# A Fourier-mixing and squared-ReLU kernel: other weights for the pieces of the next transform, products and helpers issued at other places

## The chip, the cores and the metric

The kernel runs on one core of a Trainium2 chip. Its engines are TensorE (matrix products), VectorE and GpSimd (elementwise work), ScalarE (activations and copies) and SyncE, whose queue (SP's) starts most transfers. Each engine works through its own list of instructions in order and waits on semaphores for the others. The metric is the time on the device in microseconds; lower is better.

## The reference

The input x has 8 sequences of 3008 rows and 256 columns. Each is transformed by a two-dimensional Fourier transform of which the real part is kept; the rows that result go through a feed-forward layer with a squared ReLU:

```python
X = np.fft.fft(x, axis=1)
X = np.fft.fft(X, axis=2)
y = X.real.reshape(8 * 3008, 256)
h = y @ w_in              # 256 x 2048
r = np.maximum(h, 0.0)
out = (r * r) @ w_out     # 2048 x 256
```

## The kernel before

**The transform of a sequence** uses symmetry. Rows n, S-n, M-n and M+n are loaded together (`load_x`), and `fold` adds and subtracts them on VectorE in five pieces: `f_s`, `f_d`, `f_sc`, `f_dc` and `f_w`, and for three of the eight tiles a sixth, a reversal of the partitions. Pairs of tiles are then halved further by turns (`once`, `twice`): copies and scaled copies on ScalarE (`begin`, `sine`, `copies`) and sums on VectorE (`even`, `odd`, `turned`, `odd_v`, `odd_w`). What the turns multiply by lies in the small tile `turn`, made by `make_turn` from columns of the tables of cosines and sines. Last come four groups for each sequence (`dft_ops`, `group`; part P or Q, even or odd columns). Each has a product `even_n` on TensorE, joins on VectorE, a second product `odd_n`, and `join_1`, which writes Pt or Qt. The products go to PSUM tiles `pd` of a pool with two buffers, which `even_n` and `odd_n` use in turn, so an `even_n` may start when the group before has joined the even half. ScalarE copies part of a product to SBUF ahead of each join.

One column of every transform (E) is treated apart. `load_column` fetches it for sequences 1 to 7 during steps 8 to 14 in 28 small transfers, `fold_columns` doubles it on ScalarE and folds it on VectorE into `we`, and a pass of two groups, `dft_ops(None)`, transforms it; the result is stored to `e_dram` and later broadcast to Et (`load_e`). After this pass `part_table` reorders the columns of four tables on ScalarE; the pass needs the old order, the groups of sequences 1 to 7 the new one.

**The main loop** goes through 384 steps: 8 sequences, 6 blocks of 251 (the last 250) columns, and 8 steps j in each. A step's `front` makes, for two halves h, two products into PSUM `ph` (two buffers; L763 and L764) and from these on VectorE `he` and both sides of `g` (L766, L768, L769); `combine` applies ReLU and square on ScalarE (L778, L779) and makes four sums s on GpSimd (L786 to L789). `back` makes seven products from g and s into accumulators in PSUM, two steps later (LAG is 2). The first eight steps are of a plainer form, and w_out is converted during them. After a block's last step `gather` combines the accumulators, and `store` transposes and stores in two later steps.

**The next sequence's transform is woven in.** `ahead(b + 1)` lists its pieces, each with a cost. After each half of a front `between` is called. It lowers `spent` by `pace` (the sum of costs by the number of calls; a quarter of it before step 16), and then issues pieces while `spent` is not above zero, adding their costs:

```python
while side and spent <= 0:
    t, f = side.pop(0)
    f()
    spent += t
```

Nothing is issued in the first ten steps nor in steps with i % 8 == 1. An issued piece stands in its engines' queues behind what was issued before it: a product issued in the first half's call stands on TensorE between the two halves of that front, a piece for VectorE right after that half's g. So the costs decide in which half step a piece stands and nothing else. In sequence 0 there are 53 calls, later 78.

Of the kernel before, what the change touches and what calls it, by code (L numbers as in the profile page):

```python
# [82 lines left out]
def kernel(  # L83
# [12 lines left out]
    nc = tc.nc  # L96
    B, NROW, _, D = x.shape
# [6 lines left out]
    NJ = NFC // 2  # L104
# [33 lines left out]
    ODD0 = NT - 3  # L138
    TWO = ODD0 - 2
# [44 lines left out]
    cosT = const.tile([P, 2, WT], F32, name="cosT")  # L184
    sinT = const.tile([P, 2, WT], F32, name="sinT")
# [150 lines left out]
    turn = const.tile([P, 3, 4], F32, name="turn")  # L336
    BY_AC, BY_BD, BY_TWO, BY_AB = range(4)

    def make_turn():


        for i, t, kp, k in ((BY_AC, ODD0, 1, 0), (BY_TWO, TWO, 1, 0), (BY_AB, ODD0, 0, 1)):
            for a, tab in enumerate((cosT, sinT, sinT)):
                r = slice(0, ROWS2)
                nc.scalar.mul(turn[r, a, i:i + 1], tab[r, kp, PLACE[t] + k:PLACE[t] + k + 1], -1.0 if a == 2 else 1.0)
        c, z = (turn[0:ROWS2, a, BY_AC:BY_AC + 1] for a in range(2))
        for a, (u, v, op) in enumerate(((c, z, ALU.add), (c, z, ALU.subtract), (z, c, ALU.subtract))):
            to = turn[0:ROWS2, a, BY_BD:BY_BD + 1]
            tt(out=to, in0=u, in1=v, op=op)
            nc.scalar.mul(to, to, 0.5 ** 0.5)  # L350
# [35 lines left out]
    def load_column(t):  # L386

        _, r0, step, rows = TILES[t]
        for i in range(4):
            nc.sync.dma_start(out=xe[0:rows, i, t], in_=x[1:B, r0:r0 + step * (rows - 1) + 1:step, i, H].rearrange("b r -> r b"))  # L390

    def fold_columns():
        nc.scalar.mul(xe, xe, 2.0)
        s = hp.tile([P, 2, NT, NE], F32, name="es", tag="es", bufs=1)
        tt(out=s, in0=xe[:, 0::2], in1=xe[:, 1::2], op=ALU.add)
        for kp in range(2):
            tt(out=we[:, kp], in0=s[:, 0], in1=s[:, 1], op=ALU.subtract if kp else ALU.add)
# [3 lines left out]
    def fold(b, t):  # L401


        odd, two = b > 0 and t >= ODD0, b > 0 and t == TWO + 1
        r = slice(0, ROWS2 if odd or two else TILES[t][3])
        st = {}

        def new(pool, nm, shape):
            st[nm] = pool.tile(shape, F32, name=nm, tag=nm)
            return st[nm]  # L410

        def f_s():
            nonlocal folds
            st["fs"] = sums[folds % 2]
            folds += 1
            v = xt[b, t]
            tt(out=st["fs"][r, :, 0:D], in0=v[r, 0::2], in1=v[r, 1::2], op=ALU.add)

        def f_d():
            v = xt[b, t]  # L420
            tt(out=new(fp, "fd", [P, 2, D])[r], in0=v[r, 0::3], in1=v[r, 1:3], op=ALU.subtract)
            if b > 0:
                load_later(b * NL + ORDER.index(t) + NX)

        def halves():

            if b == 0 or "sc" not in st:
                st["sc"] = fp.tile([P, 2, D], F32, name="sc", tag="sc")
            return st["sc"]

        def f_sc():
            s = st["fs"]
            tt(out=halves()[r, :, PART[0]], in0=s[r, :, 0:H + 1], in1=s[r, :, D:H - 1:-1], op=ALU.add)

        def f_dc():
            d = st["fd"]
            tt(out=halves()[r, :, PART[1]], in0=d[r, :, 1:H], in1=d[r, :, D - 1:H:-1], op=ALU.subtract)

        def w_of(t):
            if (b, t) not in folded:  # L440
                folded[b, t] = wp.tile([P, 2, D], F32, name="w", tag="w")
            return folded[b, t]

        def f_w(part=slice(0, D)):
            v, w = st["sc"], w_of(t)
            for kp in range(2):
                tt(out=w[r, kp, part], in0=v[r, 0, part], in1=v[r, 1, part], op=ALU.subtract if kp else ALU.add)

        def f_e():
            nc.scalar.mul(lone[r, 2 * t:2 * t + 2, P - 1:], w_of(t)[r, :, H:H + 1], -1.0 if TILES[t][0] else 1.0)  # L450

        if b == 0:
            return [f_s, f_d, f_sc, f_dc, lambda: (f_w(PART[0]), f_e()), lambda: f_w(PART[1])]
        ops = [(0.9, f_s), (0.9, f_d), (0.7, f_sc), (0.6, f_dc), (1.1, f_w)]
        if odd and (t - ODD0) in (1, 2) or two:
            ops.append((0.7, lambda: nc.vector.stream_shuffle(w_of(t)[r], w_of(t)[r], REVERSE)))
        return ops

    def spare(nm):
# [77 lines left out]
    def dft_ops(b):  # L537
# [7 lines left out]
        def group(kp, which):  # L545
# [168 lines left out]
            if b == 0:  # L714
# [3 lines left out]
                    for nm, f in (("even", even_part), ("odd", odd_part)):  # L718
                        named += [(nm + ("", "_e")[e] + str(i), lambda i=i, e=e, f=f: f(i, e == 1)) for e in range(2)]
                return [((which, kp, nm), f) for nm, f in named]  # L720
            ops = [(0.1, even_n), (0.4, join_4), (0.5, join_2), (0.1, odd_n), (0.8, join_1)]
            if b and kp:
                ops.insert(4, (0.5, lambda: join_odd("odd", n0)))
                ops.insert(2, (0.4, lambda: join_odd("half", n1)))
            elif b:
                ops.insert(4, (0.4, join_turned))
            return ops

        ops = [] if b is None else [(0.0, start)]
# [19 lines left out]
    def load_e(b):  # L749
        nc.sync.dma_start(out=PQE[b][2], in_=e_dram[b:b + 1].to_broadcast([P, NKT]))  # L750
# [137 lines left out]
            nc.sync.dma_start(out=rows[full * R:], in_=part[R - rest:, full])  # L888

    def ahead(b):  # L890
        start, *groups = dft_ops(b)
        if b == 1:

            tables = [(0.3, lambda tab=tab, t=t: part_table(tab, t)) for t in (TWO, ODD0) for tab in (cosT, sinT)]
            groups = [(1.5, fold_columns)] + dft_ops(None) + tables + groups
        def woven(ops, chain):

            chain = list(chain)
            out = []
            for i, x in enumerate(ops):  # L900
                out += [x] + ([chain.pop(0)] if chain and i else [])
            return out + chain

        av, aw, bv, bw = range(ODD0, NL)

        def later(make):

            made = []

            def run(i):  # L910
                if not made:
                    made.extend(make())
                made[i]()

            return lambda times: [(x, lambda i=i: run(i)) for i, x in enumerate(times)]

        w = lambda t: folded[b, t]
        two = later(lambda: once(w(TWO), w(TWO + 1), BY_TWO))((0.1, 0.9, 0.2, 1.0))
        first = later(lambda: once(w(av), w(aw), BY_AC))((0.1, 0.9, 0.2, 1.0))
        second = later(lambda: once(w(bv), w(bw), BY_BD) + twice(w(av), w(aw), w(bv), w(bw)))(  # L920
            (0.1, 0.9, 0.2, 1.0, 0.1, 1.2, 0.2, 1.2, 0.2, 0.9, 0.9))
        return (fold(b, TWO) + fold(b, TWO + 1) + woven(fold(b, 0), two) + fold(b, av) + fold(b, aw)
                + woven(fold(b, bv), first) + fold(b, bw) + woven(fold(b, 1), second)
                + [start] + groups + [(0.0, lambda: load_e(b))])

# [95 lines left out]
    def between():  # L1023


        nonlocal spent
        if i < NJ + LAG or i % NJ == LAG - 1:
            return
        spent -= pace / 4 if i < 2 * NJ else pace
        while side and spent <= 0:  # L1030
            t, f = side.pop(0)
            f()
            spent += t

    late = []

# [20 lines left out]
    for i in range(len(steps) + LAG + 4):  # L1057
        if i < len(steps):
            b, k0, n, j = steps[i]
            if i == NJ:  # L1060
                for k in range(NX):
                    load_later(NL + k)
            if NJ <= i < NJ + NT:
                load_column(i - NJ)
            if i == NJ:
                make_turn()
            if i % per == 0:
                assert not side
                side = ahead(b + 1) if b + 1 < B else []
                calls = 2 * (NJ - 1) * (len(BLOCKS) - (0 if i else 2)) - 6 + (0 if i else (NJ - LAG) // 2)  # L1070
                spent, pace = 0.0, sum(t for t, _ in side) / calls
            g = front(b, k0, n, j, between)
            if i < NJ:
                weights()
                s = combine(n, g, True)
            elif i < 2 * NJ:
                leftover()
                sum_wout(j)
        while finished and finished[0][0] <= i:
            store(*finished.pop(0)[1:])  # L1080
        if i >= LAG and flight:
            at, g_, s_ = flight.pop(0)
            final = at[:3] == (B - 1, *BLOCKS[-1])
            back(at[2], at[3], g_, s_, final)
            if at[3] == NJ - 1:
                c_ = gather(at[2], s_ is None, final)
                finished += [(i + 2 + s, *at[:3], s, c_, final) for s in range(2)]
        if i + 1 < NJ:
            late.append(win[i + 1][2]())
            leftover()  # L1090
        if i < len(steps):
            flight.append(((b, k0, n, j), g, s if i < NJ else combine(n, g, False)))
# [63 lines left out]
```

## Time and profile before

| what | value |
|---|---|
| median of 3 runs | 1939.22 us (1937.83 to 1939.67) |
| the profiled execution | 1939.15 us |
| its span, first to last instruction | 1937.4 us |
| mean granted clock of TensorE | 0.998 |
| busy: TensorE, VectorE, GpSimd, ScalarE | 1916.4, 1498.2, 1178.7, 957.4 us |
| TensorE busy from 300 to 400 us | 100.00 us |

Step 8 begins at about 98 us, step 48 (sequence 1) at about 312 us, and each later sequence of 48 steps takes some 231 us. A line of the timeline gives the start in us, the duration, the engine, the line of the kernel, what is written from what, and in brackets how long the engine stood idle before it and for whom. TensorE's matmuls are pipelined: two that are shown with 0.59 us follow the next pair after 0.425 us. A list of waits gives the waiting engine and line, for whom, the total in us, how often, and the longest.

### The profile page before, as it was taken

The numbers are of one execution on the slowest core, as the hardware profiler recorded it, in microseconds if no ns is written. First come the engines' busy times: TensorE is split into PE (matmuls) and PEld (weight loads), VectorE is DVE, ScalarE is ACT, GpSimd is POOL, SyncE is SP. The second block draws the span as 40 slices with busy tenths as digits, with TensorE's granted clock in tenths as the row PEclk, the third lists the DMA queues.
The fourth block names the chain that finished last, engine by engine and source line by source line (L and its number), as shares of the span: only waits on it lengthen the run. The fifth ranks groups of instructions, "written<-read, shape, count | busy, mean of one in ns | idle before, by whom it ended". The sixth has DMA issues, their size and how long they took to land.

```text
span 1937.4 us, 28151 instructions
## 1 busy us (share of the span) xinstructions
PE 1916.4 (99%) x9266; PEld 1699.7 (88%) x9266; DVE 1498.2 (77%) x3657; ACT 957.4 (49%) x1201; POOL 1178.7 (61%) x1701
## 2 busy tenths in 40 slices
PE   8999999999999999999999999999999999999998
PEld 7788878888988889888988889888898888988887
DVE  8989967888778886888868887788877788655554
ACT  2845544455445454544544455445544455444443
POOL 0047645667566765676556766676756676556655
PEclk9999999999999999999999999999999999999999
DMA  8331102111111111111011210121112101100101
GB/s 216 115 37 44 40 8 52 30 28 32 33 29 36 31 27 27 36 31 43 12 36 29 45 28 11 37 45 28 28 17 49 35 12 22 27 12 11 22 11 23
DMA packets 145786, 69.58 MB, mean 36 GB/s; under 512 B 129309, under 2 KB 136423, under 8 KB 145638
## 3 DMA queue, kind: packets, MB, share of 16 engines
q1 hardware_dynamic: 145186, 66.87, 15.9%
q8 instruction: 73, 1.20, 0.3%
q14 instruction: 75, 0.61, 0.1%
q0 software_dynamic: 176, 0.65, 0.1%
q10 hardware_dynamic: 276, 0.26, 0.0%
HBM read 43.03 MB, written 24.69 MB: 35 GB/s over the span
## 4 chain that ended last, share of the span: by engine, by line
PE 93%; DVE 4%; DMA 1%; SPq 1%; issue 1%; ACT 0%; POOL 0%; DVEq 0%; POOLq 0%
PE mA L816 16%; PE mC L816 16%; PE mB L816 16%; PE ph L763 16%; PE ph L764 16%; PE mD L816 8%; PE pd L564 2%; PE pd L666 1%; PE pd L640 1%; DVE he L766 1%; DVE g L769 0%; DMA cosT<-in_cos_s_dram 0%; DVE m L284 0%; DVE g L768 0%; DVE fd L282 0%
## 5 line engine op out<-in xcount | busy, mean ns | idle before, releaser
L778 ACT ACTIVATE g<-g 128x1004 f32<-128x1004 f32 (+1 forms) x384 | 399.3, 1040 | 747.3 <-DVE g L769 315.6
L786 POOL TENSOR_TENSOR s<-g 128x251 f32<-128x251 f32 (+1 forms) x376 | 244.8, 651 | 652.7 <-ACT g L779 574.1
L766 DVE SCALAR_TENSOR_TENSOR he<-Et,gE,ph 128x251 f32<-128x251 f32 (+1 forms) x768 | 359.8, 468 | 314.5 <-PE ph L764 312.7
L763 PE MATMUL ph<-Pt,G 128*128 128x251 f32 (+1 forms) x1536 | 452.6, 376 | 3.5 <-DVE g L769 3.4
L764 PE MATMUL ph<-Qt,G 127*128 127x251 f32 (+1 forms) x1536 | 451.7, 375 | 0.0
L779 ACT ACTIVATE g<-g 128x1004 f32<-128x1004 f32 (+1 forms) x384 | 399.3, 1040 | 12.2
L816 PE MATMUL mC<-s,wsum 128*128 128x251 f32 (+1 forms) x1504 | 381.7, 375 | 0.0
L816 PE MATMUL mA<-g,wout 128*128 128x251 f32 (+1 forms) x1504 | 381.6, 375 | 0.0
L768 DVE TENSOR_TENSOR g<-he,ph 128x251 f32<-128x251 f32 (+1 forms) x768 | 320.5, 417 | 52.9 <-ACT g L778 0.5
L764 PEld LDWEIGHTS ph<-Qt,G 127*128 127x128 f32 x1536 | 291.5, 190 | 35.9
L763 PEld LDWEIGHTS ph<-Pt,G 128*128 128x128 f32 x1536 | 286.4, 189 | 40.3 <-DVE g L769 5.8
L816 PEld LDWEIGHTS mC<-s,wsum 128*128 128x128 f32 x1504 | 285.6, 190 | 34.7
L769 DVE TENSOR_TENSOR g<-he,ph 128x251 f32<-128x251 f32 (+1 forms) x768 | 314.2, 409 | 0.0
L816 PEld LDWEIGHTS mA<-g,wout 128*128 128x128 f32 x1504 | 281.8, 189 | 35.4 <-issue 1.3
L787 POOL TENSOR_TENSOR s<-s,g 128x251 f32<-128x251 f32 (+1 forms) x376 | 292.0, 776 | 29.5
L788 POOL TENSOR_TENSOR s<-g 128x251 f32<-128x251 f32 (+1 forms) x376 | 294.4, 783 | 0.0
L789 POOL TENSOR_TENSOR s<-g,s 128x251 f32<-128x251 f32 (+1 forms) x376 | 257.8, 686 | 0.0
L816 PE MATMUL mB<-g,wsum 128*128 128x251 f32 (+1 forms) x752 | 220.7, 374 | 0.0
L816 PE MATMUL mD<-s,wout 128*128 128x251 f32 (+1 forms) x752 | 220.3, 374 | 0.0
L816 PE MATMUL mB<-s,wout 128*128 128x251 f32 (+1 forms) x752 | 219.9, 374 | 0.0
L816 PEld LDWEIGHTS mB<-g,wsum 128*128 128x128 f32 x752 | 142.9, 190 | 17.5
L816 PEld LDWEIGHTS mD<-s,wout 128*128 128x128 f32 x752 | 141.9, 189 | 17.7
(152 smaller groups left out, 1442.3 us busy)
## 6 DMA issues: line engine op xcount, KB each, us to landing
out_dram<-os SPq DMA_DIRECT2D x376, 56.0 KB
xt<-in_x_dram SPq DMA_DIRECT2D x39, 384.0 KB
xt<-in_x_dram SPq DMA_DIRECT2D x63, 128.0 KB
Et<-e_dram SPq DMA_DIRECT2D x7, 752.5 KB
out_dram<-os SPq DMA_DIRECT2D x288, 6.8 KB
raw<-in_moe_w_in_dram SPq DMA_DIRECT2D x16, 256.0 KB
raw<-in_moe_w_out_dram SPq DMA_DIRECT2D x16, 256.0 KB
xt<-in_x_dram SPq DMA_DIRECT2D x2, 512.0 KB
```

Of the source, the lines that this page charges most:

```text
L763: nc.tensor.matmul(hP, G1[:, fs], pt[:, ks], start=True, stop=True)
L764: nc.tensor.matmul(hQ, G2[0:P - 1, fs], qt[0:P - 1, ks], start=True, stop=True)
L766: nc.vector.scalar_tensor_tensor(out=t, in0=et[:, ks], scalar=gE[:, fc:fc + 1], in1=hP, op0=ALU.mult, op1=ALU.add)
L768: tt(out=g[:, h, 0, 0:n], in0=t, in1=hQ, op=ALU.add)
L769: tt(out=g[:, h, 1, 0:n][:, ::-1], in0=t, in1=hQ, op=ALU.subtract)
L778: act(v, v, AF.Relu)
L779: act(v, v, AF.Square)
L786: gt(out=s1, in0=g21, in1=g22, op=ALU.add)
L787: gt(out=s2, in0=s1, in1=g11, op=ALU.subtract)
L788: gt(out=s3, in0=g11, in1=g21, op=ALU.subtract)
L789: gt(out=s4, in0=g12, in1=s2, op=ALU.subtract)
L816: nc.tensor.matmul(acc[nm][:, i, 0:n], w, v[:, 0:n], start=j == 0 and i == 0, stop=j == NJ - 1, skip_group_check=True)
```

## The change

The costs of the pieces are replaced by others. Pieces of cost zero are no longer counted: `between` issues them right after the piece ahead of them, in the same call, and ends its counted loop at them. The products `even_n` and `odd_n` and the ScalarE helpers of the turns (`begin`, `sine`, `copies`), which had 0.1 or 0.2, now have zero. `make_turn` is split: `take_turn` takes the nine factors, `make_turn` does the rest, and both stand at the head of sequence 1's list in place of step 8's start. The doubling of E's column becomes a piece of its own, and it, the fold, the pass for E and the four tables, which stood between the turns and the groups, now stand between the folds of the tiles av and aw, in the middle of the list. The tables have cost zero.

```diff
-    def make_turn():
+    def take_turn():
         for i, t, kp, k in ((BY_AC, ODD0, 1, 0), (BY_TWO, TWO, 1, 0), (BY_AB, ODD0, 0, 1)):
             for a, tab in enumerate((cosT, sinT, sinT)):
                 r = slice(0, ROWS2)
                 nc.scalar.mul(turn[r, a, i:i + 1], tab[r, kp, PLACE[t] + k:PLACE[t] + k + 1], -1.0 if a == 2 else 1.0)
+
+    def make_turn():
         c, z = (turn[0:ROWS2, a, BY_AC:BY_AC + 1] for a in range(2))
...
+    def scale_columns():
+        nc.scalar.mul(xe, xe, 2.0)
+
     def fold_columns():
-        nc.scalar.mul(xe, xe, 2.0)
         s = hp.tile([P, 2, NT, NE], F32, name="es", tag="es", bufs=1)
...
-        ops = [(0.9, f_s), (0.9, f_d), (0.7, f_sc), (0.6, f_dc), (1.1, f_w)]
+        ops = [(1.0, f_s), (0.9, f_d), (0.6, f_sc), (0.6, f_dc), (1.3, f_w)]
         if odd and (t - ODD0) in (1, 2) or two:
-            ops.append((0.7, lambda: nc.vector.stream_shuffle(w_of(t)[r], w_of(t)[r], REVERSE)))
+            ops.append((0.8, lambda: nc.vector.stream_shuffle(w_of(t)[r], w_of(t)[r], REVERSE)))
...
-            ops = [(0.1, even_n), (0.4, join_4), (0.5, join_2), (0.1, odd_n), (0.8, join_1)]
+            ops = [(0.0, even_n), (0.5, join_4), (0.8, join_2), (0.0, odd_n), (1.2, join_1)]
             if b and kp:
-                ops.insert(4, (0.5, lambda: join_odd("odd", n0)))
-                ops.insert(2, (0.4, lambda: join_odd("half", n1)))
+                ops.insert(4, (0.7, lambda: join_odd("odd", n0)))
+                ops.insert(2, (0.5, lambda: join_odd("half", n1)))
             elif b:
-                ops.insert(4, (0.4, join_turned))
+                ops.insert(4, (0.5, join_turned))
...
-        start, *groups = dft_ops(b)
+        (_, start), *groups = dft_ops(b)
         if b == 1:
 
-            tables = [(0.3, lambda tab=tab, t=t: part_table(tab, t)) for t in (TWO, ODD0) for tab in (cosT, sinT)]
-            groups = [(1.5, fold_columns)] + dft_ops(None) + tables + groups
+            tables = [(0.0, lambda tab=tab, t=t: part_table(tab, t)) for t in (TWO, ODD0) for tab in (cosT, sinT)]
+            early = [(0.0, start), (0.0, take_turn), (0.5, make_turn)]
+            middle = [(0.0, scale_columns), (2.0, fold_columns)] + dft_ops(None) + tables
+        else:
+            early, middle = [], []
+            groups = [(0.0, start)] + groups
...
-        two = later(lambda: once(w(TWO), w(TWO + 1), BY_TWO))((0.1, 0.9, 0.2, 1.0))
-        first = later(lambda: once(w(av), w(aw), BY_AC))((0.1, 0.9, 0.2, 1.0))
+        two = later(lambda: once(w(TWO), w(TWO + 1), BY_TWO))((0.0, 1.1, 0.0, 1.5))
+        first = later(lambda: once(w(av), w(aw), BY_AC))((0.0, 1.1, 0.0, 1.5))
         second = later(lambda: once(w(bv), w(bw), BY_BD) + twice(w(av), w(aw), w(bv), w(bw)))(
-            (0.1, 0.9, 0.2, 1.0, 0.1, 1.2, 0.2, 1.2, 0.2, 0.9, 0.9))
-        return (fold(b, TWO) + fold(b, TWO + 1) + woven(fold(b, 0), two) + fold(b, av) + fold(b, aw)
+            (0.0, 1.1, 0.0, 1.5, 0.0, 1.2, 0.0, 1.4, 0.0, 1.1, 1.1))
+        return (early + fold(b, TWO) + fold(b, TWO + 1) + woven(fold(b, 0), two) + fold(b, av) + middle + fold(b, aw)
                 + woven(fold(b, bv), first) + fold(b, bw) + woven(fold(b, 1), second)
-                + [start] + groups + [(0.0, lambda: load_e(b))])
+                + groups + [(0.0, lambda: load_e(b))])
...
-        while side and spent <= 0:
+        while side and side[0][0] and spent <= 0:
             t, f = side.pop(0)
             f()
             spent += t
+        while side and not side[0][0]:
+            side.pop(0)[1]()
...
-            if i == NJ:
-                make_turn()
```

## The prediction

> **What bounds the kernel now.** First the page's busy times, then the busy time of each engine in stretches of the run.
>
> ```profile
> PE 1916.4 (99%) x9266; PEld 1699.7 (88%) x9266; DVE 1498.2 (77%) x3657; ACT 957.4 (49%) x1201; POOL 1178.7 (61%) x1701
> ...
> 160.00:200.00 40.00, 39.50 (x186) 34.78 (x186) 37.42 (x86) 21.89 (x28) 27.32 (x37) 1.00 0.21 53
> 200.00:244.00 44.00, 42.45 (x198) 36.81 (x196) 41.50 (x98) 23.62 (x37) 28.37 (x40) 1.00 0.18 37
> 244.00:300.00 56.00, 53.28 (x270) 43.76 (x271) 38.55 (x110) 24.99 (x44) 23.69 (x37) 0.97 0.10 25
> ...
> 486.00:600.00 114.00, 114.00 (x568) 102.34 (x567) 85.13 (x215) 53.94 (x67) 71.40 (x104) 1.00 0.13 29
> 728.00:970.00 242.00, 242.00 (x1179) 216.41 (x1178) 191.90 (x466) 120.16 (x148) 156.88 (x224) 1.00 0.14 30
> ```
>
> The columns after the length are TensorE matmuls, weight loads, VectorE, ScalarE and GpSimd, then the granted clock. TensorE sets the time. From 300 us to the last sequence it has no idle time at all, so whatever the change does to the six later transforms can only cost. Only in the first sequence, up to about 300 us, is anything to be won; there VectorE is at 94% (41.50 of 44 us) and TensorE has holes. The chain of waits for TensorE names them:
>
> ```profile
> PE ph L763 <- DVE g L769: 3.4, 4, 1.6
> ...
> PE pd L564 <- DVE we L397: 2.7, 1, 2.7
> ...
> PE pd L564 <- DVE dc L608: 0.3, 1, 0.3
> ```
>
> Four waits for VectorE's g and one for the columns we. The timeline shows the two large ones. Near 104 us, where `make_turn` stands ahead of step 8's front:
>
> ```profile
> 102.83 1.04 ACT L779 ACTIVATE g<-g 128x1004 f32<-128x1004 f32 x1
> ...
> 103.77 0.19 ACT L345 ACTIVATE turn<-cosT 96x1 f32<-96x1 f32 x1
> ...
> 104.08 0.30 DVE L349 TENSOR_TENSOR turn<-turn 96x1 f32<-96x1 f32 x3 [3.96 <-ACT turn L345]
> 104.30 0.47 DVE L766 SCALAR_TENSOR_TENSOR he<-Et,gE,ph 128x251 f32<-128x251 f32 x1
> ...
> 105.60 0.69 PE L763 MATMUL ph<-Pt,G 128*128 128x251 f32 x2 [1.57 <-DVE g L769]
> ...
> 107.58 1.04 PE L764 MATMUL ph<-Qt,G 127*128 127x251 f32 x2
> ```
>
> VectorE sits 3.96 us for nine ScalarE factors that queue behind the squares; TensorE waits 1.57, then runs at half rate (1.04 where 0.59 is usual). And at 246 us:
>
> ```profile
> 245.21 0.43 DVE L395 TENSOR_TENSOR es<-xe 128x98 f32<-128x98 f32 x1
> ...
> 245.67 1.38 DVE L397 TENSOR_TENSOR we<-es 128x49 f32<-128x49 f32 x2
> ...
> 246.43 1.63 PE L564 MATMUL pd<-cosT,we 95*7 95x95 f32 x8 [2.67 <-DVE we L397]
> ...
> 247.99 2.04 PE L816 MATMUL mA<-g,wout 128*128 128x251 f32 x4
> ```
>
> The same again: 2.67 idle, then 2.04 for four matmuls that take 1.01.
>
> **What the Trainium skill says.** "TensorE: Matmul & The Clock Gate", Part 1, What's actually happening: the array falls to half clock after an idle window of about 3.4 us and needs as long a busy stretch to recover. The trace agrees on the recovery (slow until 110.5 and 250.5, some 4 us each) but differs on the trigger: 1.57 us was enough, while the 1.04 us at 237 was not. Same page, Architectural detail: ScalarE and VectorE are strict FIFOs, and TensorE may pull only weight loads forward; the 3.96 us, with step 8's front stuck behind L349, is that. "SBUF — State Buffer", two separate sides: VectorE with two SBUF inputs and GpSimd exclude each other; L492, always 94x256, runs from 0.474 to 0.934 us here, so traced costs of pieces scatter by a factor of two.
>
> **Where the pieces go.** The costs are only weights in the planner's count; they change positions, no instruction. For b=1 the sum before is 33.6 (eight folds of 4.2) + 2.1 (shuffles) + 11.3 (turns) + 1.5 + 3.8 (pass for E) + 1.2 (tables) + 10.2 (groups) = 63.7; after 35.2 + 2.4 + 12.6 + 0.5 + 2.0 + 5.0 + 0 + 13.4 = 71.1. Over 53 calls the pace is 1.202 and 1.342; the first 12 (steps 10 to 15) count a quarter. fold_columns has 47.0 ahead of it before: (47.0-12x0.3005)/1.202 = 36.1, so the 37th full call, first half of step 37; its products come a call later. After: 21.5 ahead, (21.5-4.02)/1.342 = 13.03, the 14th full call, second half of step 23, and as even_n now costs 0 it is issued **in the same call**. Likewise the last turn piece, and with it the first product of sequence 1, falls in step 38. For b>1: 57.2 and 63.6 over 78, pace 0.733 and 0.815; nothing overruns.
>
> **Part by part**, in TensorE time, counted between issues (a matmul pair is 0.425 us).
>
> 1. make_turn leaves step 8. The last issue before the hole ends at 103.87; six pairs (2.55) later would be 106.42, but it is 110.50. Lost 4.1, all of it freed unless something else is late next: the conversion of wout that the products need (0.68+0.69+0.69 behind two fronts of 1.2 from 100.1) ends near 104.6, before its use at 105.6. I take 4.1; the ends are 1.7 (idle alone) and 4.1. The factors come back in step 10: nine ScalarE copies (0.84 traced) then three subtractions (0.3) and three ScalarE scalings (0.37). ScalarE has a 1.25 us gap there. VectorE may wait some 0.6 for them with the first fold queued behind, and is 0.9 later through steps 11 to 15, where it does 4.77 us a step by its fronts against TensorE's 4.675. Cost 0.5 at step 16 (0 to 1.4).
> 2. The pass for E leaves step 37: lost from 243.49 (h1's last issue end) to 250.51. Of this 2.94 is the wait, and 1.73 the slow clock (products 1.56 for the 1.07 of the second pass's, mA 1.84 for 0.85, mB 0.68 for 0.425). Freed 4.7.
> 3. It arrives in step 23. There TensorE's front starts at 174.63 and both halves are issued by 1.70 later. VectorE starts that front 1.0 late (176.27 against 174.63+0.63), then needs front 1.22, f_w of av 1.11, front 1.24, and es and the first we 1.17 less 0.06: we is ready 0.63+1.0+4.68 = 6.3 after the step's start. Wait 4.6, against 2.94 before: the call of slack is gone. With the slow clock at its old 1.73: 6.3. Without any lag 5.3; with 2 us lag and a full slow window more, 8.3. The moved step's other instructions: the xe scaling on ScalarE (0.35, a call earlier, so done by 177.8 before VectorE asks); 28 column loads, issued by 144.9, so they have landed; 28 products (same count); the E store on SP's queue, behind which only stores of steps 27 and 28 stand; twelve table copies on ScalarE, now in one call of step 26. They took 3.7 us traced (260.64 to 264.33) beside half-idle ScalarE; the pair g and s of that step is used two steps (9.35 us) later and needs about 5. Hidden; without that cover up to 2.
> 4. The folds after it: 22 calls instead of 23 before the turns are done. The bunch of four butterflies and turned products (2.81 and 1.13 traced at 233 to 238, which cost the waits of 1.04 and 0.27) stays in adjacent calls, and the one at 166 (0.50) too: taken as unchanged, 2.6 in all; ends 0 and 4.
> 5. Groups: the 0.46 at 288 goes, but the second product group in step 39 now needs join_2 of the call before: TensorE ready 0.85+0.86+0.85 = 2.56 after the step's start, join_2 done near 0.63+1.24+1.16 = 3.0: 0.45 back. Net 0.
> 6. Later sequences: join_4 no longer stands in the call of its product, so VectorE waits less; VectorE bounds nothing there. The same PSUM reuse occurs twice in each (six sequences): join_2 alone is 0.62, so done at 2.50, against 2.56. Zero; ends 0 and 0.5 each.
>
> Sum: -4.1 + 0.5 - 4.7 + 6.3 = **-2.0 us**. The profiled execution is 1939.15 (span 1937.4, 1.75 around it), the median of the runs 1939.22: forecast **1937.2 us**. A change is told from none here at about 0.2%, 3.9 us.
>
> **Rivals.**
> - *Both holes close.* If VectorE reaches step 23 without lag (wait 3.6, sum 5.3) and real weights also spread the bunches (-2.6): -4.1+5.3-4.7-2.6 = -6.1, 1933.1. For it: weights come closer to traced times (f_s 0.96 in later sequences, was 0.9; join_1 1.1, was 0.8). Against: VectorE's total work in the first sequence is the same and near full.
> - *Slower: a product in TensorE's queue before its PSUM buffer is free.* Place: the second and fourth product group of every sequence, in the call after the join_2 that releases the buffer, with matmuls strictly in order behind it. Each us that VectorE is late counts fully, twelve times. Above 0.17 us each (12x0.17 = 2.0) it outweighs the forecast, at 0.5 it gives +4.0, at 0.8 +7.6 (1946.7). Against: before that call VectorE has 4.5 us of work in a step of 5.5.
> - *The make_turn gain doesn't arrive*: VectorE, not TensorE, paces steps 9 to 22, so that only 1.7 comes and stalls at 16 and 21 take 2.0: -1.7+2.0-4.7+7.3 = +2.9, 1942.0.
>
> **Chances.** Forecast as summed 0.48, both holes 0.25, PSUM order 0.12, no gain from make_turn 0.15. Faster by over 0.2% needs -3.9: the second case and a little of the first, 0.27. Slower by over 0.2%: most of the third case and a third of the last, plus a worse stall at step 23, 0.19. Within: 0.54. The likeliest case alone spans 1935 to 1940; the range that holds the rivals down to the last fifth is 1933.0 to 1944.0.
>
> **What would show it.** Right: no VectorE wait for turn near 100 us and matmuls of 0.59 from 99 to 110; the wait of TensorE for we grows from 2.7 to about 4.4 us and moves to around 170 us, with half-rate matmuls after it; stretches from 300 us on still without TensorE idle. Wrong: the wait for we under 3, a new row of pd waiting for joins with a count of twelve, or waits for VectorE's g above 3.

## The result and the profile after

The changed kernel takes 1951.67 us (median of 4 runs, 1949.55 to 1954.28) where the kernel before takes 1939.45: a ratio of 1.0064, 95% interval 1.0046 to 1.0081. It is slower, where 1937.2 us was forecast with a range of 1933.0 to 1944.0. The profiled executions are 1953.37 and 1939.15 us, their spans 1951.6 and 1937.4: 14.2 us apart, and it is these that the sums below explain. The profiled execution of the changed kernel is one of two that took some 4 us more than the other two, at a mean granted clock of 0.996 against 0.999, so its half-rate stretches need not be in every run.

The busy times of the changed kernel and two of its stretches (TensorE, weight loads, VectorE, ScalarE, GpSimd, clock):

```profile
PE 1925.7 (99%) x9266; PEld 1701.7 (87%) x9266; DVE 1510.8 (77%) x3657; ACT 952.6 (49%) x1201; POOL 1185.4 (61%) x1701
...
160.00:200.00 40.00, 35.13 (x148) 26.36 (x147) 26.07 (x62) 14.80 (x20) 17.75 (x26) 0.91 0.11 24
728.00:970.00 242.00, 241.44 (x1169) 214.90 (x1169) 191.78 (x464) 117.25 (x145) 157.91 (x224) 1.00 0.14 31
```

The stretch in which TensorE had no idle time before, 728 to 970 us, now has 0.56 us of it. By the starts of their first fronts, each of the six later sequences takes 232.74 us where it took 231.43. The waits of TensorE after the change (engine and line, for whom, total, times, longest):

```profile
PE ph L765 <- DVE g L771: 4.7, 6, 1.2
PE pd L566 <- DVE we L399: 3.5, 1, 3.5
...
PE pd L566 <- DVE dc L612: 2.1, 7, 0.8
PE pd L566 <- DVE dc L610: 1.7, 6, 0.3
PE pd L668 <- DVE Qt L610: 1.6, 1, 1.6
```

L765 and L771 are L763 and L769 of before. The last three rows are new in kind or in number: products into `pd` that wait for joins, 14 times where it was once. Laid out by place, with the half-rate matmuls that follow a long wait counted in (read off the starts of successive matmuls against the usual 0.425 us a pair):

| TensorE time lost, us | before | after |
|---|---|---|
| step 8, the factors | 4.1 | 0 |
| folds up to step 23, waits for g | 0.8 | 3.8 |
| the pass for E | 4.6 | 6.7 |
| folds and turns after it, waits for g | 1.8 | 3.0 |
| products of sequence 1's groups, waits for dc and Qt | 0.6 | 4.7 |
| six later sequences | 0 | 6 x 1.31 = 7.8 |
| sum | 11.9 | 26.0 |

The difference, 14.1, agrees with the 14.2 between the spans. By the starts of the fronts, 6.8 us are lost between steps 8 and 48 and 7.8 after that, and the start-up before step 8 was 0.5 shorter.

One of the longer waits for g comes after step 18 of the changed kernel:

```profile
148.78 0.93 DVE L435 TENSOR_TENSOR sc<-fs 96x258 f32<-96x258 f32 x1
149.63 0.84 DVE L439 TENSOR_TENSOR sc<-fd 96x254 f32<-96x254 f32 x1
150.50 1.59 DVE L449 TENSOR_TENSOR w<-sc 96x256 f32<-96x256 f32 x2
...
153.31 0.69 PE L765 MATMUL ph<-Pt,G 128*128 128x251 f32 x2 [1.14 <-DVE g L771]
```

f_sc, f_dc and f_w all stand in one call, between the two halves of the step. The new costs allow that: 0.6 and 0.6 together are under the pace of 1.342, so a third piece can follow, while the old 0.7 and 0.6 exceed the old pace of 1.202.

Where the pass for E stands now, in step 23:

```profile
177.56 0.41 DVE L771 TENSOR_TENSOR g<-he,ph 128x251 f32<-128x251 f32 x1
177.98 0.26 DVE L397 TENSOR_TENSOR es<-xe 128x98 f32<-128x98 f32 x1
178.27 0.33 DVE L399 TENSOR_TENSOR we<-es 128x49 f32<-128x49 f32 x2
178.54 2.06 PE L566 MATMUL pd<-cosT,we 95*7 95x95 f32 x8 [3.55 <-DVE we L399]
180.53 2.04 PE L818 MATMUL mA<-g,wout 128*128 128x251 f32 x4
182.37 1.04 PE L818 MATMUL mB<-g,wsum 128*128 128x251 f32 x2
...
184.04 1.43 PE L818 MATMUL mC<-s,wsum 128*128 128x251 f32 x4
```

The products follow the fold in the same call, so TensorE stands idle for 3.55 us in front of them, and after that runs at half rate until about 185 us. And one of the new waits, in step 84 of the changed kernel, at the second product group of a later sequence:

```profile
487.75 0.58 PE L765 MATMUL ph<-Pt,G 128*128 128x251 f32 x2
488.80 0.48 DVE L768 SCALAR_TENSOR_TENSOR he<-Et,gE,ph 128x251 f32<-128x251 f32 x1 [0.76 <-PE ph L766]
489.97 0.35 DVE L608 TENSOR_TENSOR dc<-db,pd 128x189 f32<-128x189 f32 x1
490.23 0.34 DVE L612 TENSOR_TENSOR dc<-db,pd 128x188 f32<-128x188 f32 x1
490.72 0.65 PE L566 MATMUL pd<-cosT,w 95*128 95x94 f32 x4 [0.21 <-DVE dc L612]
```

VectorE begins the front 1.05 us after TensorE's first issue, because its first instruction waits for both products (L766 in the bracket), not for the one it reads. join_2 (L608, L612) ends at 490.57, and only then may the product go that was ready at 490.34. Counted between issues this place costs 0.47 us, its twin in step 88 0.54.

The longest of the new waits is in step 43 of the first sequence, at the second product of the last group, and the matmuls after it run at half rate:

```profile
294.00 1.04 PE L668 MATMUL pd<-cosT,w 94*127 94x95 f32 x4 [1.63 <-DVE Qt L610]
```

### The profile page after: what moved, and what is told of

Read it like the earlier page. It is cut to its first block, busy times and chain, and to the rows that moved or that the text cites. A ratio compares the mean times of both kernels' runs of the same rounds, so it can differ in the third digit from the quotient of the medians.

```text
span 1951.6 us, 28139 instructions
## 1 busy us (share of the span) xinstructions
PE 1925.7 (99%) x9266; PEld 1701.7 (87%) x9266; DVE 1510.8 (77%) x3657; ACT 952.6 (49%) x1201; POOL 1185.4 (61%) x1701
## 4 chain that ended last, share of the span: by engine, by line
PE 87%; DVE 10%; issue 1%; DMA 1%; POOL 0%; SPq 0%; ACT 0%; DVEq 0%; POOLq 0%
PE mA L818 15%; PE mC L818 15%; PE mB L818 15%; PE ph L765 15%; PE ph L766 15%; PE mD L818 8%; PE pd L566 2%; DVE he L768 2%; DVE g L770 1%; DVE g L771 1%; DMA xt<-in_x_dram 1%; PE pd L668 1%; PE pd L642 1%; DVE w L449 0%; DVE w L471 0%
## 5 line engine op out<-in xcount | busy, mean ns | idle before, releaser
L788 POOL TENSOR_TENSOR s<-g 128x251 f32<-128x251 f32 (+1 forms) x376 | 243.2, 647 | 661.8 <-ACT g L781 527.1
L765 PE MATMUL ph<-Pt,G 128*128 128x251 f32 (+1 forms) x1536 | 453.8, 376 | 5.1 <-DVE g L771 4.7
L766 PE MATMUL ph<-Qt,G 127*128 127x251 f32 (+1 forms) x1536 | 451.8, 375 | 0.0
L765 PEld LDWEIGHTS ph<-Pt,G 128*128 128x128 f32 x1536 | 284.6, 189 | 45.6 <-DVE g L771 11.1
L766 PEld LDWEIGHTS ph<-Qt,G 127*128 127x128 f32 x1536 | 291.4, 190 | 35.7
L771 DVE TENSOR_TENSOR g<-he,ph 128x251 f32<-128x251 f32 (+1 forms) x768 | 314.3, 409 | 0.0
L790 POOL TENSOR_TENSOR s<-g 128x251 f32<-128x251 f32 (+1 forms) x376 | 305.3, 812 | 0.0
L789 POOL TENSOR_TENSOR s<-s,g 128x251 f32<-128x251 f32 (+1 forms) x376 | 285.5, 759 | 29.5
```

The source lines that it names most:

```text
L765: nc.tensor.matmul(hP, G1[:, fs], pt[:, ks], start=True, stop=True)
L766: nc.tensor.matmul(hQ, G2[0:P - 1, fs], qt[0:P - 1, ks], start=True, stop=True)
L771: tt(out=g[:, h, 1, 0:n][:, ::-1], in0=t, in1=hQ, op=ALU.subtract)
L788: gt(out=s1, in0=g21, in1=g22, op=ALU.add)
L789: gt(out=s2, in0=s1, in1=g11, op=ALU.subtract)
L790: gt(out=s3, in0=g11, in1=g21, op=ALU.subtract)
```

## The experiments

All runs were made beside the kernel before, which had medians of 1940.1, 1939.5 and 1939.6 us in the three groups of runs. Ratios are to it, with 95% intervals.

**The factors alone.** The kernel before, with the split and the places of the two halves (their cost is 0, so no piece moves):

```diff
+        head = fold(b, TWO)
+        if b == 1:
+            head = [(0.0, take_turn), head[0], (0.0, make_turn)] + head[1:]
...
-            if i == NJ:
-                make_turn()
```

> The kernel before with one part of the change: the factors are taken at the head of sequence 1's list (step 10) and turned into sums one piece later (step 11), nothing ahead of step 8; all costs and all other positions are those of before. Theory (TensorE paces steps 8 to 22 once the hole is closed): VectorE's wait of 4.0 us for turn and TensorE's hole of 1.57 us with the half-rate matmuls after it go, 4.1 us in all, and reach the end: 1935.3 us against 1939.4. Rival (VectorE paces this stretch): the gain is given back as waits for g before step 23, 1937.5 to 1939.5.

Measured: 1936.5 us, 0.9979 (0.9972 to 0.9987). The wait for turn is gone. By the starts of the fronts, 4.1 us are won by step 10, 0.7 of it is given back by step 22 (0.4 in step 21, where the wait for g grows from 0.50 to 0.91), and 3.4 us reach step 48 and the end. The theory holds, less that 0.7; this part of the change is a gain.

**Products counted again.** The changed kernel, with one line for the groups of the sequences:

```diff
+            own = 0.1 if b else 0.0
-            ops = [(0.0, even_n), (0.5, join_4), (0.8, join_2), (0.0, odd_n), (1.2, join_1)]
+            ops = [(own, even_n), (0.5, join_4), (0.8, join_2), (own, odd_n), (1.2, join_1)]
```

> The changed kernel, but even_n and odd_n of the sequences' own groups cost 0.1 again, so that they are counted and come a call or more later; the pass for E keeps its zeros. By the planner's count the product that needs a buffer is then two calls or more after the join that frees it in sequence 0 and three or more in the later ones, where it was one. Theory (a product one call after that join waits for it): waits of pd for dc and Qt go from 14 to at most 2; 1.0 us a sequence in the six later ones and about 4.9 us in the first are freed, 10 to 11 us of the 14: 1940 to 1942 us where the changed kernel has 1951.7. Rival (the other costs and the shifted positions are what costs, through VectorE): 1947 or more, with the waits gone but waits for g grown.

Measured: 1946.0 us, 1.0030 (1.0019 to 1.0041). Its waits:

```profile
PE ph L766 <- DVE g L772: 6.5, 15, 1.2
PE pd L566 <- DVE we L399: 3.1, 1, 3.1
...
PE pd L566 <- DVE db L612: 0.3, 1, 0.3
```

Half of each: the waits of pd for dc and Qt are gone, as the theory has it, and 5.6 us with them, but the waits for g went from 6 to 15, and the later sequences still lose 0.7 to 1.25 us each. The other pieces had shifted with the pace, so this run mixes two things.

**The fold ahead of the pass.** The changed kernel, with the doubling and the fold two steps earlier:

```diff
-            middle = [(0.0, scale_columns), (2.0, fold_columns)] + dft_ops(None) + tables
+            lead = [(0.0, scale_columns), (2.0, fold_columns)]
+            middle = dft_ops(None) + tables
...
-        return (... woven(fold(b, 0), two) + fold(b, av) + middle + ...
+        return (... woven(fold(b, 0), two) + lead + fold(b, av) + middle + ...
```

> The changed kernel, but the doubling and the fold of E's column stand ahead of the fold of av, two steps before the products that need them, and no longer in the same call. Theory (the products stand in TensorE's queue ahead of their input's making): the wait for we of 3.5 us and the half-rate matmuls after it, 6.7 us together, go: 1945 to 1946 us. Rival (VectorE is behind anyway and the stall only takes another name): waits of ph for g grow by as much before step 27, 1950 or more.

Measured: 1946.7 us, 1.0041 (1.0028 to 1.0054); the profiled execution is 7.3 us below that of the changed kernel, the medians are 5.0 apart. By the starts of the fronts the 6.7 us of the theory are won in step 23; the rest of the 7.3 is start-up. The wait for we is gone; the waits for g are the same 4.7 us in 6. The theory holds, though the median lies 0.7 us above the range.

**The new costs alone.** The kernel before, with the new numbers for VectorE's pieces (products 0.1, helpers 0.1 and 0.2 as before, nothing moved):

```diff
-        ops = [(0.9, f_s), (0.9, f_d), (0.7, f_sc), (0.6, f_dc), (1.1, f_w)]
+        ops = [(1.0, f_s), (0.9, f_d), (0.6, f_sc), (0.6, f_dc), (1.3, f_w)]
-            ops = [(0.1, even_n), (0.4, join_4), (0.5, join_2), (0.1, odd_n), (0.8, join_1)]
+            ops = [(0.1, even_n), (0.5, join_4), (0.8, join_2), (0.1, odd_n), (1.2, join_1)]
...
```

> The kernel before with the new costs alone for all VectorE pieces; products and helpers keep their 0.1 and 0.2, are counted as before, and nothing is moved in the list. Theory (what hurts is products in the call after, or the same as, their cause): in no sequence is a product one call after the join that frees its buffer, and E's products come two calls or more after their fold, so no wait for we or dc; the later sequences lose at most the 0.33 us each at the turn of tile 0: 1934 to 1940 us. Rival (the weights spoil the order): 1943 or more, with waits for g in every sequence.

Measured: 1947.5 us, 1.0035 (1.0023 to 1.0047). A miss: the rival won. No product into `pd` waits for Qt, dc or we, one waits 0.2 us for db, and still 7.4 us are lost. What is lost to g is more than that, since the wait for we with its half-rate matmuls, 4.6 us in the kernel before, is gone here too:

```profile
PE ph L763 <- DVE g L769: 8.2, 14, 1.9
```

By the starts of the fronts 6.4 us are lost in the six later sequences; in the first, one wait of 1.90 us in step 36 is followed by half-rate matmuls that cost 3.3 more. The timeline of a later sequence in this run shows how:

```profile
338.52 0.59 PE L763 MATMUL ph<-Pt,G 128*128 128x251 f32 x2
...
339.99 0.79 DVE L437 TENSOR_TENSOR sc<-fd 96x254 f32<-96x254 f32 x1
340.81 1.68 DVE L447 TENSOR_TENSOR w<-sc 96x256 f32<-96x256 f32 x2
342.42 0.46 DVE L766 SCALAR_TENSOR_TENSOR he<-Et,gE,ph 128x251 f32<-128x251 f32 x1
342.76 0.59 PE L764 MATMUL ph<-Qt,G 127*128 127x251 f32 x2
343.71 0.48 PE L763 MATMUL ph<-Pt,G 128*128 128x251 f32 x1 [0.36 <-DVE g L769]
```

f_dc and f_w stand together between the two halves of step 53 and take VectorE 2.46 us, so g of the second half, and with it the buffer of `ph`, is late for the first product of the next step's second half. How much the gap between the halves holds can be worked out: VectorE starts 1.05 after the step's first issue, each half takes 1.24, and TensorE wants the buffer of the second half at 4.675 + 0.85 = 5.53; 5.53 - 1.05 - 2 x 1.24 leaves 2.0 us for pieces between the halves. In sequence 1 the half steps of this run with 2.46, 2.19 and 1.99 us between the halves are followed by waits of 0.52, 0.26 and 0.05; the run with counted products has 2.29 (0.34), 2.45 (0.51) and 2.01 (0.06), the changed kernel 2.16 (0.22). The wait is what exceeds 1.95; by the starts of the fronts each costs some 0.1 more, since the first pair after a wait takes 0.53 instead of 0.425. In the kernel before no first half of sequence 1 holds more than 1.95 where TensorE has no other work, and none waits. After the second half, 2.7 us passed without a wait. In the first sequence VectorE often begins a front later than 1.05, and the room is smaller by that: in step 18 of the changed kernel it begins on time and has 3.24 us between the halves (wait 1.14), in step 21 it begins at 1.97 and has 2.78 (wait 1.25).

**Both large holes closed in the kernel before.** The factors moved as in the first run, and

```diff
-            groups = [(1.5, fold_columns)] + dft_ops(None) + tables + groups
+            lead = [(1.5, fold_columns)]
+            groups = dft_ops(None) + tables + groups
...
-                + woven(fold(b, bv), first) + fold(b, bw) + woven(fold(b, 1), second)
+                + woven(fold(b, bv), first) + lead + fold(b, bw) + woven(fold(b, 1), second)
```

> The kernel before with the factors moved to step 10 as in the first of these runs, and the doubling and fold of E's column set ahead of the fold of bw (step 29), eight steps before its products, which stay in step 37. All costs and the counting are those of before. Theory: both large holes go, 3.6 to 4.1 and 4.6 us, and nothing else moves by more than a call: 8 to 9 us under the kernel before of the same chip, about 1931. Rival (VectorE is full, the second stall takes another name): 4 us under it, with waits of ph for g grown by about 4.

Measured: 1931.99 us, 0.9962 (0.9949 to 0.9974), 7.5 below the kernel before, where 8 to 9 were expected, and the best of all runs. The wait for we is gone. What TensorE waits for g:

```profile
PE ph L763 <- DVE g L769: 3.3, 3, 1.7
```

The kernel before has 3.4 us there, but 1.57 of it is the hole at the factors. Without that the waits for g grew from 1.8 to 3.3, so part of the rival came true: of the 8.7 us in the two holes 6.7 arrive, by the starts of the fronts. The longest wait, 1.70 near 241 us, follows four instructions (`turned`, L521) that take 2.50 us here, between the halves of step 36, and 1.13 in the kernel before. Why the same instructions take so much longer is not shown; the prediction's explanation of such a scatter, that VectorE and GpSimd exclude each other, was tested by no run.

**Only the odd-column product later.** The changed kernel, with a cost that is above zero and counts nothing, so that this product alone moves to the call of its own join:

```diff
+            own = 1e-6 if b and kp else 0.0
+            ops = [(own, even_n), (0.5, join_4), (0.8, join_2), (0.0, odd_n), (1.2, join_1)]
```

> The changed kernel, but even_n of the odd-column groups has a cost of a millionth: it is then issued with its own join_4 and no longer in the call of join_1 before, and no other piece changes its place. Theory (a product one call after the join that frees its PSUM buffer waits): the 13 waits of pd for dc go, 1.0 us in each later sequence and 1.2 in the first, 7.2 together, to about 1944 to 1945 where the changed kernel has 1951.7; per later sequence the loss against before falls from 1.33 to 0.33. Rival (VectorE is late at this place and TensorE would wait for g instead, as it did when all products were counted): 1949 or more, with the loss per later sequence unchanged.

Measured: 1945.0 us, 1.0025 (1.0016 to 1.0034), 6.7 below the changed kernel. The 13 waits for dc are gone, and between steps 48 and 96 it loses 0.25 us to the kernel before where the changed kernel loses 1.32. Of that difference 0.98 falls in steps 84 and 88 and 0.09 in step 57, the step after the densest gap. With VectorE's pieces all in their places, the PSUM buffer's price is about 1.0 us a sequence.

**All those products later.** `own` for both products and both kinds of group:

> The changed kernel with a cost of a millionth for every even_n and odd_n of the sequences' own groups: each is issued with the join that follows it, VectorE's pieces stay where they are. Theory: as with the even_n of the odd columns alone, and the wait of pd for Qt at step 43 (odd_n one call after join_1) goes too with its half-rate matmuls, 3.7 us more: 1940 to 1942. Rival: VectorE now waits for the products inside a call and pays it back as waits for g: 1946 or more.

Measured: 1942.05 us, 1.0013 (1.0006 to 1.0019). The wait for Qt is gone too; the waits for g are still 4.7 us in 6, so VectorE does not pay it back.

**The same with the fold ahead.**

> The same with the doubling and fold of E's column ahead of the fold of av as well. Theory (the losses add up): the changed kernel's 14.2 us over before in its profiled execution less 7.3 for the fold (as measured in the run with the fold ahead) less 10.9 for the products: 4 us under the kernel before, 1935 to 1937. Rival: as in the run before, 1941 or more.

Measured: 1935.83 us, 0.9982 (0.9974 to 0.9989). The losses add up. This kernel still has the new costs, and is 3.8 us above the one with both holes closed under the old: by the starts of the fronts 2.2 in the first sequence and 1.5 in the later ones.

**One butterfly moved.** The run before, with other costs for two pieces of tile 0 in sequences 2 to 7:

```diff
+        c, d = (0.9, 0.3) if t == 0 and b > 1 else (0.6, 0.6)
-        ops = [(1.0, f_s), (0.9, f_d), (0.6, f_sc), (0.6, f_dc), (1.3, f_w)]
+        ops = [(1.0, f_s), (0.9, f_d), (c, f_sc), (d, f_dc), (1.3, f_w)]
```

> The repaired kernel of the run before, but in sequences 2 to 7 the costs of f_sc and f_dc of tile 0 are 0.9 and 0.3 in place of 0.6 twice: only the butterfly of its turn moves, from the call of f_sc (first half of step 56) to the next call. Theory (VectorE starts 1.05 us after the first issue of a front and needs 1.24 for each half, so more than 2.0 us of pieces between the halves makes TensorE wait; here 2.13 were traced): the loss of 0.25 us per later sequence goes to 0.0, 1.5 us together, 1934 to 1935. Rival (that loss has another cause, such as GpSimd's hold on the port): unchanged, 0.25 a sequence, 1935.8.

Measured: 1934.3 us, 0.9973 (0.9963 to 0.9983). Between steps 48 and 112 the run before lost 0.49 us to the kernel before, this one loses 0.01. The bound of 2.0 us between the halves holds where it was put to the test.

**More calls for the first sequence.** The kernel with both holes closed, and

```diff
-                calls = 2 * (NJ - 1) * (len(BLOCKS) - (0 if i else 2)) - 6 + ...
+                calls = 2 * (NJ - 1) * (len(BLOCKS) - (0 if i else 2)) - (6 if i else 2) + ...
```

> The kernel with the factors moved and the fold ahead, and in sequence 0 four more calls to spread the pieces over (57 for 53, pace 1.118 for 1.202), so that they end in step 46 instead of 44. Theory (the waits for g that are left in the first sequence, 3.3 us, come from VectorE's pieces standing too densely): they fall by 1 to 3 us, to 1929 to 1931 where that kernel has 1932.0. Rival (they come from single dense calls, not from the pace; or the last groups now crowd the end and Et is late for step 48): 1932 or more.

Measured: 1933.25 us, 0.9968 (0.9957 to 0.9980): no gain. The waits for g are still four (1.05, 0.73, 0.31 and 1.28 us), at other steps. They go by single dense calls, as the rival has it, and not by the pace.

## Why the prediction was wrong, by its own steps

- *Part 1, the factors*: right. 4.1 freed and 0.5 back were forecast; by the starts of the fronts it was 4.1 and 0.7, in the medians 3.6 in sum.
- *Parts 2 and 3, the pass for E leaves step 37 and arrives in step 23*: right in mechanism, and nearly in sum, by two errors that cancel. Freed 4.7, measured 4.6. Added 6.3, measured 6.7: the wait between issues was 3.7, not 4.6, since es and the first we took about 0.56 us instead of 1.17; the half-rate matmuls after it cost 3.0, not 1.7, as they lasted until 185 us. That second part varies: after the same wait in the run with all those products later they cost 1.8.
- *Part 4, the folds after it, "taken as unchanged, 2.6 in all"*: this step failed first. The losses at waits for g in the first sequence are 6.8 us, up 4.2. The prediction went by which pieces stand in adjacent calls, and not by how much stands between the two halves of one step. The timeline of before would have given the limit: 2.40 us between the halves of step 20 and 2.81 in step 35 are followed by its waits of 0.50 and 1.04. The run with the new costs alone shows the same kind of loss without any other part of the change, though at other steps. That the new order is the cause of the whole 4.2 in the changed kernel is argued from the runs that take its other losses away.
- *Part 5, groups, "Net 0"*: failed. The wait in step 39 came with 1.1 us (0.45 forecast). The one in step 43 was overlooked: odd_n of the last group stands one call after the join_1 that frees its buffer, and costs 3.6 with its half-rate matmuls. The prediction had only the even products for this pair.
- *Part 6, later sequences, "Zero; ends 0 and 0.5 each"*: failed by one term. join_2 was put at 2.50 us after the step's start against 2.56 for TensorE, with VectorE starting at 0.63, the end of the first product. It starts at 1.05, after the second. That gives 1.05 + 1.24 + 0.62 = 2.91, so 0.35 late, and 0.47 and 0.54 were measured. Both ends of the range were there; the wrong one was taken. The page of the kernel before shows it: VectorE's he waits for L764, not for L763. Twelve places at about 0.5 are 6 us.

```profile
L766 DVE SCALAR_TENSOR_TENSOR he<-Et,gE,ph 128x251 f32<-128x251 f32 (+1 forms) x768 | 359.8, 468 | 314.5 <-PE ph L764 312.7
```

So the rival of a product ahead of its PSUM buffer came true, at its place and with its count, and the price at which it was said to give +4.0. It carries 6 of the 14.2 us, in the later sequences. It did not come because VectorE was late, as that rival assumed, but because the normal time of VectorE was misread; and it came together with the dense half steps, which no rival named. The third rival had the place of those in the first sequence, with another cause: of the 4.1 us that the factors free, 1.0 is left at step 23 of the changed kernel. With the old costs 3.4 are left there (the factors alone), so it is the order of the pieces and not VectorE's pace that takes them. And the first rival's hope that costs nearer to the traced times spread the bunches came out the other way.

## What to carry to other kernels

Before work is woven between two dependent streams, work out from the trace how much each gap holds (here 2.0 us between the halves when VectorE is on time, more after the second) and keep each call under it; an average pace, even of traced durations, doesn't see it. A product issued early is free only if its input and its buffer are free when an in-order TensorE reaches it: count the calls to the join that releases the buffer, and treat one call as a wait. Read the start of a consumer from what its rows say that it waits for, not from the operand that it uses.

## What was not expected of the hardware

TensorE fell to half rate after idle stretches of 1.57 and 2.67 us (the kernel before), 1.63 and 3.55 (the changed kernel) and 1.90 (the new costs alone), and not after those of 1.04, 1.25 and 1.30 (the last in the run with only the odd-column product later). In between, the length alone does not decide. In the kernel with both holes closed a stretch of 1.70 us left the rate as it was:

```profile
240.64 0.69 PE L763 MATMUL ph<-Pt,G 128*128 128x251 f32 x2 [1.70 <-DVE g L769]
241.17 0.59 PE L764 MATMUL ph<-Qt,G 127*128 127x251 f32 x2
```

So did one of 1.56 us in the run with the new costs alone, at the very place of the 1.57 of the kernel before. What decides there stays open. The slow stretch varied too: in the changed kernel it ran for about 6.5 us after the wait of 3.55, in the run with all those products later for about 4 after one of 3.56. A trimmed wait may therefore save twice: with only the odd-column product later, that wait in step 43 fell by 0.33 us, and the 1.7 us of the slow stretch behind it did not come. That is one execution, and the trimming need not be the reason.
